# A depthwise convolution with an MLP behind it: how W_in is loaded and cast at the start, and how the taps are spread over the partitions

## The chip, the cores and the metric

One core of one Trainium2 chip. The metric is the device time of one execution in microseconds (us). The engines are named as the profile names them: PE is TensorE (matmuls; PEld its weight loads), DVE is VectorE, ACT is ScalarE, POOL is GpSimd, SP is SyncE, which here only issues DMAs. ACT issues some DMAs too. SPq and ACTq in the trace are those issues.

## The reference

```python
def _attn_ref(x, weight):                 # x [8, 4096, 192], weight [8 heads, 7 taps]
    w = np.exp(weight - max over the taps)
    w = w / (np.sum(w, axis=-1, keepdims=True) + 1e-09)
    x_pad = 6 zero rows ahead of x in each sequence
    out[b, s, h*24 + g] = sum over k of w[h, k] * x_pad[b, s + k, h*24 + g]

def _moe_ref(x, w_in, w_out):             # x [32768, 192], w_in [192, 2048], w_out [2048, 192]
    h = x @ w_in
    g = 0.5 * h * (1.0 + erf(h / sqrt(2)))
    return g @ w_out
```

So each of 8 heads has 7 softmaxed taps, shared by its 24 channels; the causal convolution's result goes through two matrix products with an exact GELU between them.

## The kernel before

The 32768 tokens are cut into two halves of 16384, and the halves run side by side: token half 0 on partitions 0 to 63, half 1 on partitions 64 to 127. The 192 channels lie on those 64 partitions in three groups p = 0, 1, 2 (channel 3i + p on partition i). The tokens of a half are walked in blocks n: six of 256 tokens and then blocks of 512 (`WS`). For a block, 4 DMAs bring x (`load`), DVE transposes it in 32x32 squares (`trans`, L533), the convolution makes `xc` in bf16, PE multiplies by W_in in chunks of 128 columns (`mm1`, L774; in a block of 256, 8 units of two chunks for both halves), ACT takes the GELU of a unit (L694, tile `gT`), and PE multiplies by W_out (`mm2`, L805, and `mm2_t`, L836). PE's order is written out by hand: the `mm2` of block n-1 stand between the `mm1` of block n. `mm1` writes two buffers `hp` by turns, so unit u waits for the GELU of unit u-2.

Blocks 0 and 1 (`PC`) have their convolution on PE: `dg` holds the taps as 7 diagonal 64x64 matrices, and `pconv` (L724) adds up 7 matmuls per group into PSUM; there are four such groups, kinds 0 to 3. ACT and DVE copy the result to `xc` (`conv_out`, L191 and L193). From block 2 on the convolution is on DVE (L559, L566), with `wcol`, the taps as one column of 7 per partition, and from there on DVE works a block ahead of PE.

**W_in.** `win` (bf16) must hold, on each partition half, all 2048 columns. Each half's DMAs bring only 1024 of them, in fp32, into `winf`: half 0 columns 0 to 1023, half 1 columns 1024 to 2047. The 1024 are cut into four quarters s of 256 (`FP`). A DMA `win_in(e, s, hf)` (L234) brings a quarter of one half: 64 partitions with three rows of 256 fp32 each (1 KB), 192 KB. SP issues the four of half 0, ACT the four of half 1; each quarter has a semaphore `S_WIN[s]`, which is at 32 when both halves' DMAs have landed. `own(e, s)` (L222) casts a quarter from `winf` to `win` on all 128 partitions: quarter 0 on DVE (it counts in `S_DUPE`), quarters 1, 2 and 3 on POOL (`S_OWN`). `dup(s, hf)` (L509) on DVE then copies the cast quarter of one half to the other half's partitions, for the columns that it did not load. In block 0 the units 0 to 3 of `mm1` wait for the casts of quarters 0 to 3 and the units 4 to 7 for the doubled ones.

**The order around it.** SP issues the taps' DMA, two loads of block 0's x, four of W_in, the four loads of block 1, four of W_out (`wout_in`), the loads of blocks 2 and 3, and so on. ACT: a dummy Exp (which loads its table), two loads of block 0, the Exp of the taps, a dummy Gelu (L635, which loads that table), four loads of W_in, the casts of block 0 to bf16 (L643), its conv_outs, and then the GELUs. POOL: the identity `idb`, block 0's halo, casts 1 to 3 of W_in, block 1's halo and casts (`cast`, L206), four casts of W_out (`wcast`, L231), and then halos. DVE: the taps, the transposes of block 0, cast 0 of W_in, two conv_outs, the doubling of quarters 0 and 1, the transposes of block 1, the doubling of quarters 2 and 3, block 1's conv_outs, and from there the convolutions.

**The taps.** One DMA (L888) brings `weight` to 64 partitions, each head's 7 taps on 8 of them (a step of 0 in its source). DVE takes the negative maximum (L482), ACT the Exp with its sum (L628), DVE adds 1e-9 (L486), takes the reciprocal (L488) and multiplies (L491, twice, once per half) into `wcol`; L496 makes `dg` from `idb` and `wcol`.

**Block 1's convolution on PE.** `behind` puts 28 of its matmuls behind unit 4 of block 0 and 28 behind unit 5.

Of the kernel before, what the change touches and what calls it, by code (L numbers as in the profile page):

```python
# [11 lines left out]
def bass_lightweight_conv__then__act_gelu_exact_kernel(  # L12
# [84 lines left out]
    def sbt(name, shape, dt):  # L97
        return es.enter_context(nc.sbuf_tensor(name, shape, dt))
# [4 lines left out]
    def sem(name):  # L103
        return es.enter_context(nc.semaphore(name))

    def ap(t, off, pat):
        return bass.AP(t, off, pat)

    with es:
        win = sbt("win", [128, NP * F], BF16)  # L110
        wout = sbt("wout", [128, NF * C], BF16)
        wsb = sbt("wsb", [64, KS], F32)
        wmx = sbt("wmx", [64, 1], F32)
        wsm = sbt("wsm", [64, 1], F32)
        wrc = sbt("wrc", [64, 1], F32)
        wex = sbt("wex", [64, KS], F32)
        wcol = sbt("wcol", [128, KS], F32)
        winf = sbt("winf", [128, NP * F // 2], F32)
        woutf = sbt("woutf", [128, NF * C], F32)
        idb = sbt("idb", [128, 64], BF16)  # L120
# [11 lines left out]
        ob = pst("ob", [128, 2048])  # L132

        S_WSB = sem("S_WSB")
        S_WIN = [sem("S_WIN%d" % i) for i in range(4)]
        S_WOUT = [sem("S_WOUT%d" % i) for i in range(4)]
        S_XIN = [sem("S_XIN%d" % i) for i in range(NX)]
        S_OUT = [sem("S_OUT%d" % i) for i in range(2)]
# [74 lines left out]


        FP = [0, 256, 512, 768, FH]

        WG = [0, 4, 2, 6]

        def own(e, s):

            e.wait_ge(S_WIN[s], 32)
            return e.tensor_copy(  # L222
                ap(win, FP[s], [[NP * F, 128], [F, NP], [1, FP[s + 1] - FP[s]]]),
                ap(winf, FP[s], [[NP * FH, 128], [FH, NP], [1, FP[s + 1] - FP[s]]]),
            )
# [6 lines left out]

        def win_in(e, s, hf):
            e.dma_start(  # L234
                ap(winf, 64 * hf * NP * FH + FP[s], [[NP * FH, 64], [FH, NP], [1, FP[s + 1] - FP[s]]]),
                ap(wint, hf * FH + FP[s], [[NP * F, 64], [F, NP], [1, FP[s + 1] - FP[s]]]),
            ).then_inc(S_WIN[s], 16)

        def wout_in(e, i):
# [166 lines left out]
        @block.gpsimd  # L406
        def _(g):
            g.wait_ge(S_MSET, 1)
            for hf in range(2):
                m = idb[64 * hf : 64 * hf + 64, :]  # L410
                g.affine_select(
                    out=m,
                    in_=m,
                    compare_op=ALU.is_equal,
                    fill=0.0,
                    base=0,
                    pattern=[[-1, 64]],
                    channel_multiplier=1,
                ).then_inc(S_IDN)

            def halo(n):
                if n == 0:

                    t = xTb[0]
                    g.memset(
                        ap(t, 0, [[NP * XB, 128], [XB, NP], [32, HB]]), 0.0
                    ).then_inc(S_HALO)
                    for p in range(NP):
                        g.wait_ge(S_TR, p + 1)
                        g.tensor_copy(  # L430
                            ap(t, p * XB + 1, [[NP * XB, 128], [32, HB], [1, 31]]),
                            ap(
                                xT[0],
                                p * XW + HX + WS[0] - HL,
                                [[NP * XW, 128], [32, HB], [1, 31]],
                            ),
                        ).then_inc(S_HALO)
                    return

                t, tw = (xTb[1], XB) if n in PC else (xT[n % 2], XW)  # L440
                dst = ap(t, HF, [[NP * tw, 128], [tw, NP], [1, HB]])
                if n >= 2:
                    if n - 2 in PC:
                        wait_pc(g, n - 2, NP - 1)
                    else:
                        g.wait_ge(S_CV, cvd(n - 2))
                if OFF[n] % SEQ == 0:
                    g.memset(dst, 0.0).then_inc(S_HALO)
                    return
                g.wait_ge(S_TR, NP * n)  # L450
                if n == 1:
                    src = ap(
                        xT[0],
                        HX + WS[0] - HL + 31,
                        [[NP * XW, 128], [XW, NP], [32, HB]],
                    )
                else:
                    src = ap(
                        xT[(n - 1) % 2],
                        HF + WS[n - 1],  # L460
                        [[NP * XW, 128], [XW, NP], [1, HB]],
                    )
                g.tensor_copy(dst, src).then_inc(S_HALO)  # L463

            g.wait_ge(S_IDN, 2)
            halo(0)
            for s in range(1, 4):
                own(g, s).then_inc(S_OWN)
            halo(1)
            for p in range(NP):  # L470
                cast(g, 1, p)
            for i in range(4):
                wcast(g, i).then_inc(S_WOG)
            for n in range(2, NB):
                halo(n)

        @block.vector
        def _(v):
            v.memset(warm[:, :], 0.0).then_inc(S_WARM)  # L479
            v.memset(idb[:, :], 1.0).then_inc(S_MSET)  # L480
            v.wait_ge(S_WSB, 16)
            v.tensor_reduce(  # L482
                wmx[:, :], wsb[:, :], mybir.AxisListType.X, ALU.max, negate=True
# [3 lines left out]
            v.wait_ge(S_PRO, 2)  # L487
            v.reciprocal(wrc[:, :], wsm[:, :]).then_inc(S_PRO)  # L488
            v.wait_ge(S_PRO, 3)
            for hf in range(2):  # L490
                v.tensor_scalar(  # L491
                    wcol[64 * hf : 64 * hf + 64, :], wex[:, :], wrc[:, 0:1], None, ALU.mult
                ).then_inc(S_PRO)
            v.wait_ge(S_PRO, 5)
            v.wait_ge(S_IDN, 2)
            v.tensor_tensor(  # L496
                ap(dg, 0, [[KS * 64, 128], [64, KS], [1, 64]]),
                ap(idb, 0, [[64, 128], [0, KS], [1, 64]]),
                ap(wcol, 0, [[KS, 128], [1, KS], [0, 64]]),
                ALU.mult,  # L500
            ).then_inc(S_DG)

            def dup(s, hf):

                if s == 0:
                    v.wait_ge(S_DUPE, 1)
                else:
                    v.wait_ge(S_OWN, s)
                v.tensor_copy(  # L509
                    ap(  # L510
                        win,
                        64 * (1 - hf) * NP * F + FH + FP[s],
                        [[NP * F, 64], [F, NP], [1, FP[s + 1] - FP[s]]],
                    ),
                    ap(
                        win,
                        64 * hf * NP * F + FP[s],
                        [[NP * F, 64], [F, NP], [1, FP[s + 1] - FP[s]]],
                    ),
                ).then_inc(S_DUPE)  # L520
# [65 lines left out]

            for p in range(NP):
                trans(0, p)
            own(v, 0).then_inc(S_DUPE)
            conv_out(v, 0, 1)  # L590
            conv_out(v, 0, 4)
            for s in range(2):
                for hf in range(2):
                    dup(s, hf)
            for p in range(NP):
                trans(1, p)
            for s in range(2, 4):
                for hf in range(2):
                    dup(s, hf)
            for j in range(len(PIECES)):  # L600
                conv_out(v, 1, j)

# [18 lines left out]
        def _(a):  # L621
# [10 lines left out]
                bias=wmx[:, 0:1],  # L632
                accum_out=wsm[:, 0:1],
            ).then_inc(S_ACTP)
            a.activation(  # L635
                out=hot[:, 1:2], in_=nc.const_aps.tensor(0.0, (1, 1), F32), func=AF.Gelu
            ).then_inc(S_HOT)
            for s in range(4):
                win_in(a, s, 1)
            a.wait_ge(S_PRO, 5)  # L640
            for p in range(NP):
                a.wait_ge(S_TR, p + 1)
                a.activation(  # L643
# [61 lines left out]
        def _(t):  # L705
# [33 lines left out]
            for kd in order:  # L739
                pconv(*seq[kd].pop(0))  # L740

            behind = {
                (0, 4): [(1, kd, k) for k in taps for kd in (0, 1)],
                (0, 5): [(1, kd, k) for k in taps for kd in (2, 3)],
            }

            def mm1(n, i):
# [7 lines left out]
                    else:  # L755
                        t.wait_ge(S_CV, cvd(n))
                if n == 0:
                    if 1 <= i < 4:
                        t.wait_ge(S_OWN, i)
                    else:  # L760
                        t.wait_ge(S_DUPE, 1 if i == 0 else 2 * (i - 4) + 3)
                for cc in range(c):
                    for p in range(NP):
                        if n in PC and i == 0 and cc == 0 and p == NP - 1:
# [119 lines left out]

        @block.sync
        def _(sp):

            sp.dma_start(  # L888
                wsb[:, :], ap(wt, 0, [[KS, H], [0, 64 // H], [1, KS]])
            ).then_inc(S_WSB, 16)  # L890
            load(sp, 0, (0, 1))
            for s in range(4):
                win_in(sp, s, 0)
            load(sp, 1)
            for i in range(4):
                wout_in(sp, i)
            load(sp, 2)
            load(sp, 3)
            for n in range(1, NB):
                if n + 3 < NB:  # L900
                    load(sp, n + 3)
                store(sp, n - 1)
            for g in range(NG[NB - 1]):
                store_half(sp, g, 0)
            for s in range(2):
                sp.wait_ge(S_OUT[s], OUTS[NB - 1 if (NB - 1) % 2 == s else NB - 2])
# [28 lines left out]
```

## Time and profile before

| | |
|---|---|
| median of 6 runs | 686.67 us (686.03 to 688.16) |
| the profiled execution | 686.24 us, its span 684.5 us |
| mean granted PE clock in the span | 0.997 |
| PE busy | 676.8 us |
| L774 (mm1), busy | 420.9 us |
| L836 (mm2_t), busy | 366.3 us |
| L694 (GELU on ACT), busy | 523.3 us |
| L222 on POOL, L222 on DVE: one cast of a quarter | 0.83 us, 0.69 us |
| W_in, issue to landing, median: on SP, on ACT | 4.8 us, 6.5 us |

The groups of L774 and L836 overlap in PE's pipeline, so that their sum is more than PE's busy time. The page gives totals over the whole span; what happens in the first 30 us, which is where everything that the change touches lies, is read from the timeline and from the chain of waits. In a timeline line stand the start, the length, the engine, the line of the program, the operation, what it writes and reads, how many instructions the line stands for, and in brackets how long the engine had been idle before it and what ended that.

### The profile page before, as it was taken

What the parts mean: (1) busy time and instruction counts of PE and PEld (TensorE: products, weight loads), DVE (VectorE), ACT (ScalarE), POOL (GpSimd) and SP (SyncE); (2) the same over time, 40 slices, a digit from 0 to 9 for tenths busy, and PEclk for the clock granted to TensorE, in tenths of its full rate; (3) what the DMA queues carried; (4) which work ended last, traced back from release to release, by engine and by line L of the source; (5) the groups of instructions that cost most, each with busy time, mean ns of one, the idle gap of its engine ahead of it and who ended that gap; (6) DMA issues with size and microseconds to landing.
All of it is one profiled execution on the core that took longest, in us unless ns stands there. A gap on an engine that the chain in (4) does not pass through costs nothing.

```text
span 684.5 us, 27321 instructions
## 1 busy us (share of the span) xinstructions
PE 676.8 (99%) x12576; PEld 411.4 (60%) x12576; DVE 560.3 (82%) x902; ACT 537.2 (78%) x550; POOL 37.4 (5%) x54
## 2 busy tenths in 40 slices
PE   7999999999999999999999999999999999999998
PEld 4899755555555555555555555555555555555556
DVE  4899979888898888898888898888898888988611
ACT  5799987877777877788777877777878777778772
POOL 3224200000000000000000000000000000000000
PEclk9999999999999999999999999999999999999999
DMA  8445421244422344422344422444322444321223
GB/s 213 105 115 112 101 60 36 61 94 95 95 60 57 73 94 95 94 59 52 82 94 95 90 50 56 91 94 95 82 48 62 95 94 95 70 47 29 48 49 94
DMA packets 134363, 55.23 MB, mean 81 GB/s; under 512 B 127593, under 2 KB 134249, under 8 KB 134249
## 3 DMA queue, kind: packets, MB, share of 16 engines
q1 hardware_dynamic: 132296, 52.12, 34.7%
q8 instruction: 98, 1.61, 0.9%
q10 hardware_dynamic: 1952, 1.38, 0.8%
q14 instruction: 17, 0.13, 0.1%
HBM read 28.31 MB, written 25.17 MB: 78 GB/s over the span
## 4 chain that ended last, share of the span: by engine, by line
PE 95%; ACT 2%; DMA 1%; DVE 1%; issue 0%; POOL 0%; ACTq 0%
PE hp L774 47%; PE ob L836 42%; PE ob L805 5%; ACT gT L694 1%; DMA winf<-in_moe_w_in_dram 1%; DMA wsb<-in_weight_dram 0%; DVE xc L193 0%; PE ob L724 0%; ACT L635 0%; ACT osb L297 0%; DVE osb L339 0%; POOL win L222 0%; DVE osb L308 0%; ACT wex L628 0%; DVE wmx L482 0%
## 5 line engine op out<-in xcount | busy, mean ns | idle before, releaser
L694 ACT ACTIVATE gT<-hp 128x1024 bf16<-128x1024 f32 x512 | 523.3, 1024 | 131.5 <-PE hp L774 128.3
L774 PE MATMUL hp<-xc,win 64*64 64x512 bf16 (+2 forms) x6048 | 420.9, 366 | 2.8 <-POOL win L222 1.3
L836 PE MATMUL ob<-gT,wout 64*64 64x512 bf16 x5376 | 366.3, 376 | 0.0
L566 DVE SCALAR_TENSOR_TENSOR acc<-xT,wcol,acc 128x512 f32<-128x512 f32 (+1 forms) x495 | 314.7, 704 | 0.0
L774 PEld LDWEIGHTS hp<-xc,win 64*64 64x64 bf16 (+1 forms) x6048 | 191.0, 106 | 136.6 <-issue 1.7
L836 PEld LDWEIGHTS ob<-gT,wout 64*64 64x64 bf16 x5376 | 172.2, 118 | 122.7
L339 DVE STREAM_TRANSPOSE osb<-ob 128x512 f32<-128x512 f32 x84 | 74.0, 884 | 101.8 <-PE ob L836 101.8
L533 DVE STREAM_TRANSPOSE xT<-xin 128x512 f32<-128x512 f32 (+1 forms) x105 | 78.2, 796 | 4.0 <-DMA xin<-in_x_dram 4.0
L566 DVE SCALAR_TENSOR_TENSOR xc<-xT,wcol,acc 128x512 bf16<-128x512 f32 (+1 forms) x99 | 65.3, 717 | 0.0
L463 POOL COPY xT<-xT 128x18 f32<-128x18 f32 x30 | 27.9, 928 | 505.1 <-DVE xT L533 482.8
L805 PE MATMUL ob<-wout,gT 64*128 64x192 bf16 x1024 | 52.9, 243 | 0.3
L805 PEld LDWEIGHTS ob<-wout,gT 64*128 64x128 bf16 x1024 | 44.9, 94 | 5.2 <-PE ob L805 0.6
L559 DVE TENSOR_SCALAR acc<-xT,wcol 128x512 f32<-128x512 f32 (+1 forms) x90 | 37.6, 473 | 1.1
L310 ACT ACTIVATE osb<-ob 128x192 f32<-128x192 f32 x4 | 1.3, 332 | 9.5 <-PE ob L805 9.5
L308 DVE COPY osb<-ob 128x192 f32<-128x192 f32 x4 | 1.4, 358 | 8.4 <-PE ob L805 8.4
L708 PE MATMUL hp<-warm 128*128 128x512 bf16 x16 | 5.4, 510 | 1.3 <-DVE warm L479 1.3
L297 ACT ACTIVATE osb<-ob 128x384 f32<-128x384 f32 x12 | 5.8, 486 | 0.0
L667 ACT ACTIVATE acc<-xT,wcol 128x256 f32<-128x256 f32 (+1 forms) x9 | 5.2, 574 | 0.0
L509 DVE COPY win<-win 64x768 bf16<-64x768 bf16 x8 | 4.1, 515 | 0.9 <-POOL win L222 0.7
L708 PEld LDWEIGHTS hp<-warm 128*128 128x128 bf16 x16 | 1.9, 126 | 4.2 <-issue 2.4
L724 PE MATMUL ob<-xTb,dg 64*64 64x256 bf16 (+1 forms) x112 | 3.2, 245 | 0.5 <-ACT xTb L643 0.5
L231 POOL CAST wout<-woutf 128x768 bf16<-128x768 f32 x4 | 3.4, 870 | 1.9 <-DMA woutf<-in_moe_w_out_dram 1.9
(29 smaller groups left out, 20.2 us busy)
## 6 DMA issues: line engine op xcount, KB each, us to landing
out_dram<-osb SPq DMA_DIRECT2D x122, 192.0 KB, 3.6
xin<-in_x_dram SPq DMA_DIRECT2D x116, 192.0 KB, 4.1
xin<-in_x_dram SPq DMA_DIRECT2D x22, 96.0 KB, 5.6
woutf<-in_moe_w_out_dram SPq DMA_DIRECT2D x4, 384.0 KB, 9.0
winf<-in_moe_w_in_dram SPq DMA_DIRECT2D x4, 192.0 KB, 4.8
winf<-in_moe_w_in_dram ACTq DMA_DIRECT2D x4, 192.0 KB, 6.5
out_dram<-osb SPq DMA_DIRECT2D x8, 48.0 KB, 1.9
out_dram<-osb ACTq DMA_DIRECT2D x4, 96.0 KB, 2.0
```

The source lines that it names most:

```text
L297: e.activation(out=dst, in_=src, func=AF.Copy).then_inc(S_EVA)
L339: v.transpose(ap(osb[m % 2], j, [[8 * C, 128], [C // 2, TB // 32], [NP, 32]]), bank(ring(m, j)),).then_inc(S_EV)
L463: g.tensor_copy(dst, src).then_inc(S_HALO)
L533: v.transpose(ap(xT[n % 2], p * XW + HX, [[NP * XW, 128], [1, w]]), ap(xin[n % NX], p, [[TB // 32 * DQ, 128], [DQ, w // 32], [NP, 32]],),) ...
L559: ins = v.tensor_scalar(a, src, wk, None, ALU.mult)
L566: ins = v.scalar_tensor_tensor(dst, src, wk, a, op0=ALU.mult, op1=ALU.add)
L667: a.activation(out=acc[n % 2][:, p * TB : p * TB + w], in_=ap(xT[n % 2], p * XW + HX, [[NP * XW, 128], [1, w]]), func=AF.Copy, scale=wcol[ ...
L694: a.activation(out=ap(gT[n % 2], i * c * 2 * w, dst), in_=ap(hp[u % 2], 0, src), func=AF.Gelu,).then_inc(S_GELU)
L708: t.matmul(hp[1][:, 0:512], warm[:, 0:128], warm[:, :])
L774: ins = t.matmul(hp[u % 2][fo : fo + fw, o : o + w], ap(win, f1, [[NP * F, 64], [2, fw]]), xc[n % 2][r, p * TB : p * TB + w], start=(p == ...
L805: ins = t.matmul(bank(bb[sub], w=C), gT[m % 2][r, c0 : c0 + 128], wout[r, CH[sub][i] * C : (CH[sub][i] + 1) * C], start=(ph == 0 and i == ...
L836: ins = t.matmul(bank(ring(m, j), slice(64 * h, 64 * h + 64), w), ap(wout, 64 * hf * NF * C + CH[h][i] * C + j, [[NF * C, 64], [NP, 64]],) ...
```

## The change

- W_in comes in two parts s per half instead of four quarters: `FW` is 512 columns, so a DMA has rows of 2 KB and 384 KB in all. SP and ACT issue two each. There are two semaphores `S_WIN`; quarters 0 and 1 wait for the first, 2 and 3 for the second. On ACT the two stand ahead of the dummy Gelu instead of behind it.
- The four casts are still quarters. POOL has 0, 2 and 3 (in this order, `S_OWN`), DVE has quarter 1 (`S_DUPE`), after its two conv_outs of block 0 instead of ahead of them. The waits of `mm1` and `dup` follow.
- DVE doubles quarters 0, 1 and 2 ahead of block 1's transposes and quarter 3 behind them.
- The taps' DMA brings 8 partitions, one per head. Their softmax runs on 8 partitions, into the corner of a zeroed 32x32 tile `wnm`; a transpose makes `wnt` (taps on partitions, heads in columns), and four transposes, whose source takes each of four head columns eight times over, write `wcol` on 32 partitions each. `wcol` gets 32 columns, of which 7 are used.
- Block 1's convolution on PE stands behind units 5 and 6 instead of 4 and 5.

The core of the diff:

```diff
-        S_WIN = [sem("S_WIN%d" % i) for i in range(4)]
+        S_WIN = [sem("S_WIN%d" % i) for i in range(2)]
...
+        FW = FH // 2
...
         def own(e, s):
-            e.wait_ge(S_WIN[s], 32)
+            e.wait_ge(S_WIN[s // 2], 32)
...
         def win_in(e, s, hf):
             e.dma_start(
-                ap(winf, 64 * hf * NP * FH + FP[s], [[NP * FH, 64], [FH, NP], [1, FP[s + 1] - FP[s]]]),
-                ap(wint, hf * FH + FP[s], [[NP * F, 64], [F, NP], [1, FP[s + 1] - FP[s]]]),
+                ap(winf, 64 * hf * NP * FH + FW * s, [[NP * FH, 64], [FH, NP], [1, FW]]),
+                ap(wint, hf * FH + FW * s, [[NP * F, 64], [F, NP], [1, FW]]),
             ).then_inc(S_WIN[s], 16)
...
             halo(0)
-            for s in range(1, 4):
+            for s in (0, 2, 3):
                 own(g, s).then_inc(S_OWN)
...
+            v.memset(wnm[:, :], 0.0).then_inc(S_MSET)
...
-            for hf in range(2):
-                v.tensor_scalar(
-                    wcol[64 * hf : 64 * hf + 64, :], wex[:, :], wrc[:, 0:1], None, ALU.mult
+            v.wait_ge(S_MSET, 2)
+            v.tensor_scalar(
+                wnm[0:H, 0:KS], wex[:, :], wrc[:, 0:1], None, ALU.mult
+            ).then_inc(S_PRO)
+            v.wait_ge(S_PRO, 4)
+            v.transpose(wnt[:, :], wnm[:, :]).then_inc(S_PRO)
+            v.wait_ge(S_PRO, 5)
+            for q in range(4):
+                v.transpose(
+                    wcol[32 * q : 32 * q + 32, :],
+                    ap(wnt, 4 * (q % 2), [[32, 32], [1, 4], [0, 8]]),
                 ).then_inc(S_PRO)
-            v.wait_ge(S_PRO, 5)
+            v.wait_ge(S_PRO, 9)
...
             for p in range(NP):
                 trans(0, p)
-            own(v, 0).then_inc(S_DUPE)
             conv_out(v, 0, 1)
             conv_out(v, 0, 4)
-            for s in range(2):
+            own(v, 1).then_inc(S_DUPE)
+            for s in range(3):
                 for hf in range(2):
                     dup(s, hf)
             for p in range(NP):
                 trans(1, p)
-            for s in range(2, 4):
-                for hf in range(2):
-                    dup(s, hf)
+            for hf in range(2):
+                dup(3, hf)
...
+            for s in range(2):
+                win_in(a, s, 1)
             a.activation(
                 out=hot[:, 1:2], in_=nc.const_aps.tensor(0.0, (1, 1), F32), func=AF.Gelu
             ).then_inc(S_HOT)
-            for s in range(4):
-                win_in(a, s, 1)
-            a.wait_ge(S_PRO, 5)
+            a.wait_ge(S_PRO, 9)
...
             behind = {
-                (0, 4): [(1, kd, k) for k in taps for kd in (0, 1)],
-                (0, 5): [(1, kd, k) for k in taps for kd in (2, 3)],
+                (0, 5): [(1, kd, k) for k in taps for kd in (0, 1)],
+                (0, 6): [(1, kd, k) for k in taps for kd in (2, 3)],
             }
...
-            sp.dma_start(
-                wsb[:, :], ap(wt, 0, [[KS, H], [0, 64 // H], [1, KS]])
-            ).then_inc(S_WSB, 16)
+            sp.dma_start(wsb[:, :], ap(wt, 0, [[KS, H], [1, KS]])).then_inc(S_WSB, 16)
             load(sp, 0, (0, 1))
-            for s in range(4):
+            for s in range(2):
                 win_in(sp, s, 0)
```

More of the change, by code (lines that the diff above doesn't have):

```diff
@@ L111, in bass_lightweight_conv__then__act_gelu_exact_kernel @@
         wout = sbt("wout", [128, NF * C], BF16)
[L112 to L117, printed above, removed]
+        wsb = sbt("wsb", [H, KS], F32)
+        wmx = sbt("wmx", [H, 1], F32)
+        wsm = sbt("wsm", [H, 1], F32)
+        wrc = sbt("wrc", [H, 1], F32)
+        wex = sbt("wex", [H, KS], F32)
+        wnm = sbt("wnm", [32, 32], F32)
+        wnt = sbt("wnt", [32, 32], F32)
+        wcol = sbt("wcol", [128, 32], F32)
         winf = sbt("winf", [128, NP * F // 2], F32)
@@ L498, in _ @@
                 ap(idb, 0, [[64, 128], [0, KS], [1, 64]]),
-                ap(wcol, 0, [[KS, 128], [1, KS], [0, 64]]),
+                ap(wcol, 0, [[32, 128], [1, KS], [0, 64]]),
                 ALU.mult,
@@ L503, in dup @@
             def dup(s, hf):
-                if s == 0:
+                if s == 1:
                     v.wait_ge(S_DUPE, 1)
                 else:
-                    v.wait_ge(S_OWN, s)
+                    v.wait_ge(S_OWN, max(1, s))
                 v.tensor_copy(
@@ L757, in mm1 @@
                 if n == 0:
-                    if 1 <= i < 4:
-                        t.wait_ge(S_OWN, i)
+                    if i < 4 and i != 1:
+                        t.wait_ge(S_OWN, max(1, i))
                     else:
-                        t.wait_ge(S_DUPE, 1 if i == 0 else 2 * (i - 4) + 3)
+                        t.wait_ge(S_DUPE, 1 if i == 1 else 2 * (i - 4) + 3)
                 for cc in range(c):
```

## The prediction

> **What bounds the kernel now.** I read the page's totals first, then the chain of waits over the first 90 us, then the timeline of the first 33 us engine by engine, then a table by stage.
>
> ```profile
> span 684.5 us, 27321 instructions
> PE 676.8 (99%) x12576; PEld 411.4 (60%) x12576; DVE 560.3 (82%) x902; ACT 537.2 (78%) x550; POOL 37.4 (5%) x54
> ```
>
> TensorE (PE) works for 676.8 of 684.5 us, so 7.7 us is all that its idle time can give. The chain of waits says where it lies; columns are start, length, what:
>
> ```profile
> 0.81 2.53 DMA wsb<-in_weight_dram
> ...
> 4.03 1.17 ACT L635
> 5.20 0.03 issue
> 5.23 6.85 DMA winf<-in_moe_w_in_dram
> 12.08 0.05 issue
> 12.13 0.84 POOL win L222
> 12.97 0.14 issue
> 13.11 1.48 PE hp L774 x12
> ```
>
> Up to 13.1 us the end is set by the transfer of W_in and one cast of it on GpSimd (POOL); from 21.04 us on the chain is PE matmuls one after another. The timeline gives the PE gaps up to there in brackets: 0.48, 0.91, 0.88, 0.43, 0.17 and 0.22 us, 3.09 together. Of the rows around them:
>
> ```profile
> 8.41 0.69 DVE L222 CAST win<-winf 128x768 bf16<-128x768 f32 x1 [1.61 <-DMA winf<-in_moe_w_in_dram]
> ...
> 10.52 0.83 POOL L222 CAST win<-winf 128x768 bf16<-128x768 f32 x1 [3.32 <-DMA winf<-in_moe_w_in_dram]
> ...
> 12.13 0.83 POOL L222 CAST win<-winf 128x768 bf16<-128x768 f32 x1 [0.78 <-DMA winf<-in_moe_w_in_dram]
> ...
> 13.31 0.83 POOL L222 CAST win<-winf 128x768 bf16<-128x768 f32 x1 [0.35 <-DMA winf<-in_moe_w_in_dram]
> ```
>
> Each of the four casts starts when its quarter of W_in lands: 8.4, 10.5, 12.1, 13.3 us, so 1.63 us a quarter (393 KB), 241 GB/s. What comes behind is late for the same reason:
>
> ```profile
> 22.50 1.34 DVE L533 STREAM_TRANSPOSE xT<-xin 128x256 f32<-128x256 f32 x3 [1.52 <-DMA xin<-in_x_dram]
> ...
> 30.62 1.26 DVE L566 SCALAR_TENSOR_TENSOR xc<-xT,wcol,acc 128x256 bf16<-128x256 f32 x3
> ...
> 32.03 0.83 PE L774 MATMUL hp<-xc,win 64*128 64x256 bf16 x12
> ```
>
> Block 2's input lands at 22.50; VectorE (DVE) then works without a pause to 31.88, and PE starts that block at 32.03. The slack is 0.15 us: PE can't gain more than the landing of block 2's x gains, plus 0.15. In block 3 the slack is also small (xc done at 42.41, matmuls from 42.56). The stage table shows what the DMA engines could do (after the stretch and its length: busy PE, PEld, DVE, ACT, POOL; granted clock; DMA share; GB/s):
>
> ```profile
> 7.50:10.50 3.00, 2.09 (x66) 1.59 (x60) 2.00 (x5) 1.47 (x5) 0.00 (x0) 1.00 1.00 233
> 10.50:13.30 2.80, 1.49 (x17) 0.83 (x17) 1.01 (x3) 1.60 (x2) 1.66 (x2) 0.70 1.23 231
> 15.00:17.50 2.50, 2.33 (x53) 1.59 (x50) 2.41 (x6) 2.50 (x3) 2.15 (x5) 0.99 1.09 377
> ```
>
> W_in with its 1 KB rows moves at about 232 GB/s, W_out with 1.5 KB rows (15 to 17.5 us) at 377, both with the DMA engines full (share 1.0 and more).
>
> **The change, part by part.**
>
> *W_in in two parts of 2 KB rows.* Four issues fewer (two on SP, two on ACT, about 0.6 us each); the bytes are the same. Call T the time of one quarter's bytes, and let the first land at 8.4 minus (1.63 - T). Part A is complete one T after it, part B three T. With T 1.63 (the rate of before) A lands at 10.0 (the trace has 10.5 for its second quarter) and B at 13.3. With W_out's rate T is 393/377 = 1.04: first quarter 7.8, A 8.8, B 10.9, so 2.4 us saved at the end. A 2 KB row is longer than both, but its pitch in memory is W_in's and not the contiguous one of W_out, so I stand between: T = 1.3, A 9.4, B 12.0, 1.3 saved; the bounds are 0 and 2.4. The taps' transfer has 8 rows in place of 64. Its issue took 0.79 us and the small stores of L377 (64 rows) took 0.32 at the least; everything behind it on SP moves up by 0 to 0.47, I take 0.2. So A 9.2, B 11.8, and all that stands behind W_in on SP (x of block 1, W_out, x of block 2) lands 1.5 earlier (bounds 0 to 2.9): x of block 2 at 21.0.
>
> [...]
>
> *The taps.* Two multiplications L491 go (0.48). One multiplication on 8 rows comes (0.24) and five 32x32 transposes. The trace has no transpose of 32 columns: below it stands the smallest DVE row, 0.15, above it the 128x256 one of L533, 1.32/3 = 0.44. It is nearer to the small one: 0.18. Net 0.24 + 0.90 - 0.48 = +0.66 (0.51 to 1.96). The new memset (0.11, by L480) lies in DVE's 2.09 us wait for the taps. The taps land earlier, 0 to 0.79, I take 0.3. So dg ends at 5.9 instead of 5.56, the first transposes of x end at 7.2 instead of 6.79. On ACT the first cast waited until 6.63 though its input was there at 5.9: the four W_in issues held its sequencer until 6.53. Now two issues (to about 4.6) stand ahead of the table load (1.28 + 0.20, to 6.1), so casts start at 6.4 and the last follows the last transpose, at 7.6 (7.66 before). The convolution of block 0 ends near 8.7 as before: zero, covered by A, which lands later than that. Without cover, at 1.96, xc of block 0 would be ready at about 10.9, 0.8 on PE's path.
>
> *Casts moved.* GpSimd takes quarter 0, then 2 and 3; DVE quarter 1. On DVE the two copies to xc (9.13, 0.64) no longer stand behind a cast (0.69), so they end at 9.4. GpSimd: cast 0 from 9.2 to 10.05; 2 and 3 wait for the whole of B, 11.8 to 12.65 to 13.5. Behind these on GpSimd stand block 1's halo and casts and the W_out casts; behind cast 1 on DVE (9.4 to 10.1) the doubling copies (0.43 each) and block 1's transposes. PE then: chunk 0 at 10.1 (9.66 before), 1 at 10.8 (11.41), 2 at 12.7 (13.11), 3 at 13.6 (14.6). From here the GELU sets the pace, 1.02 each with two buffers: chunk 4 at 14.5, 5 at 15.6.
>
> *Block 1's convolution one chunk later on PE.* PE: first half 16.2 to 17.1 (0.89), chunk 6, second half to 18.3 (0.53), chunk 7 to 18.95; DVE's six copies (2.30) start at 17.1 and end at 19.3; block 1's first chunk ends at 19.65 against 21.65. PE gains 2.0. The clock: before, 12 to 15 us ran at a granted 0.50 after the gaps. If a gap at 8.7 to 10.1 does that again, chunks 2 and 3 take 1.3 instead of 0.66, some 0.6 later: gain 1.4.
>
> [...]
>
> *The sum.* PE reaches block 2 by 1.4 to 2.0 us earlier, DVE's xc by 1.5 (21.0 + 9.38 = 30.4) with 0.15 slack. W_out's last cast ends at 20.4 (21.94 - 1.5), needed at 20.6. So 1.6 us less: 686.24 (the profiled execution: span 684.5 and 1.7 around it) becomes 684.6. The median of the runs stands 0.43 above that execution, so 685.1.
>
> **The rivals.**
> 1. The saving is hidden: T stays 1.63, A 10.5, B 13.3, x of block 2 at 22.3. GpSimd's casts 2 and 3 then end at 14.1 and 15.0 (12.97 and 14.14 before), chunk 2 is a microsecond later, and the later place of block 1's convolution makes up for it: 21.5 against 21.65. 0 to 0.35 less: 686.5. For it: the DMA share is already 1.0. Against: 377 GB/s at the same share.
> 2. More: W_out's rate, T 1.04, 2.6 to 2.9 less, near the 3.09 of gaps: 683.9. Against: PE then needs W_out's last cast and DVE just as early.
> 3. Slower: the coarse wait. Casts 2 and 3 can't begin before all of B is there, and they run one after the other (0.83 each) with eight GELUs behind. By the steps above, a landing at 13.9 gives the old time and every microsecond past it costs one; from 15.3 on it is slower by more than a measurement can tell. For it: SP's x loads of block 1 are issued 1.2 us earlier and share the engines with ACT's half of B (231 GB/s with a share of 1.23 at 10.5 to 13.3). Against: the three quarters after the first would have to move at 170 GB/s (1.18 MB from 8.4 to 15.3). With B at 15.5: 688.2.
>
> **How the numbers follow.** Forecast 0.45 (its own range 684.3 to 685.8, T from 1.1 to 1.5), rival 1 0.29, rival 2 0.15, rival 3 0.11. 0.2%, about what a measurement of this kernel can tell, is 1.37 us: faster is below 685.3. That takes rival 2 and 0.37 of the forecast, 0.52; slower is rival 3 and 0.01, 0.12; the rest 0.36. The range reaches from 683.4 (all gaps gone) to 686.9 (rival 1 with a little loss).
>
> **What would show it.** Right: quarters' casts on GpSimd at about 9.2, 11.8 and 12.65; W_in above 290 GB/s; block 2's transposes at 21.0; block 1's first chunk near 19.7; PE still back to back from there. The taps' part: dg ending at 5.7 to 6.1. Wrong: x of block 2 still at 22.5 (rival 1, with a new PE gap ahead of block 2), B past 13.9 (rival 3), or transposes of 0.4 us, which would push the first convolution past A.

## The result and the profile after

| | before | after |
|---|---|---|
| median of all runs, us | 686.88 (37 runs, 685.94 to 689.27) | 688.67 (16 runs, 687.10 to 689.99) |
| the profiled execution, its span, us | 686.24, 684.5 | 687.67, 685.9 |
| PE busy / idle in the span, us | 676.8 / 7.7 | 677.1 / 8.8 |
| mean granted PE clock | 0.997 | 0.995 |

The ratio of after to before is 1.0023 with an interval of 1.0014 to 1.0031: the change costs about 1.8 us. The profiled execution of after is one of its shorter ones, 1.4 us above that of before.

The totals on the page of after:

```profile
span 685.9 us, 27323 instructions
PE 677.1 (99%) x12576; PEld 410.2 (60%) x12576; DVE 561.2 (82%) x907; ACT 537.4 (78%) x550; POOL 37.5 (5%) x54
```

PE does the same 12576 matmuls. Its idle time is 1.1 us more and its busy time 0.3 us, which is the span's 1.4. The chain of waits of after (start, length, what) says where:

```profile
3.31 10.42 DMA winf<-in_moe_w_in_dram
13.73 0.05 issue
13.79 0.84 POOL win L225
14.63 0.14 issue
14.76 4.69 PE hp L787 x48
19.45 0.95 PE ob L737 x28
```

The transfer of W_in still sets the end, and it ends at 13.73 us; before, the third quarter (the last that the chain needed) was there at 12.08. The chain's next link, one cast on GpSimd, is the same 0.84. The timeline of after, in which PE's four chunks 2 to 5 are the 4.69 us line, shows what hangs on it:

```profile
10.15 0.69 DVE L225 CAST win<-winf 128x768 bf16<-128x768 f32 x1 [1.80 <-DMA winf<-in_moe_w_in_dram]
10.18 1.08 POOL L225 CAST win<-winf 128x768 bf16<-128x768 f32 x1 [3.23 <-DMA winf<-in_moe_w_in_dram]
...
11.41 2.60 PE L787 MATMUL hp<-xc,win 64*128 64x256 bf16 x24 [3.44 <-POOL win L225]
...
13.79 1.60 POOL L225 CAST win<-winf 128x768 bf16<-128x768 f32 x2 [2.52 <-DMA winf<-in_moe_w_in_dram]
...
14.76 4.69 PE L787 MATMUL hp<-xc,win 64*128 64x256 bf16 x48 [0.75 <-POOL win L225]
...
23.23 1.34 DVE L547 STREAM_TRANSPOSE xT<-xin 128x256 f32<-128x256 f32 x3 [0.56 <-DMA xin<-in_x_dram]
...
31.34 1.27 DVE L580 SCALAR_TENSOR_TENSOR xc<-xT,wcol,acc 128x256 bf16<-128x256 f32 x3
...
33.53 0.82 PE L787 MATMUL hp<-xc,win 64*128 64x256 bf16 x12
```

Part A starts the casts at 10.15 (the prediction has 9.2), part B at 13.79 (11.8). PE's gaps are 3.44 and 0.75, 4.19 together against 3.09 before. Block 2's `xc` is done at 32.61, 0.7 us later than before, but PE takes that block up only at 33.53, 1.5 us later than the 32.03 of before: PE itself is late now, and its 1.5 is the span's 1.4. In the stage table of after (stretch and length; busy PE, PEld, DVE, ACT, POOL with their instructions; granted clock; DMA share; GB/s) stands the reason:

```profile
7.00:10.00 3.00, 0.98 (x50) 0.81 (x40) 0.63 (x2) 1.31 (x5) 0.00 (x0) 1.00 0.98 225
10.50:13.30 2.80, 1.89 (x20) 1.74 (x22) 2.03 (x5) 0.53 (x1) 0.77 (x1) 0.70 1.20 191
15.00:17.50 2.50, 2.50 (x26) 1.76 (x24) 2.43 (x5) 1.10 (x2) 1.36 (x4) 0.50 1.06 359
```

W_in with its 2 KB rows moves at 225 GB/s, no faster than with 1 KB rows (215 in the same stretch before, 233 in 7.5 to 10.5), while W_out still moves at 359. The 191 of the second row isn't the rate of W_in: in 10.5 to 13.3 us the DMA view of after has 895 packets with 0.53 MB, and 765 of them are under 512 B, rows of block 1's x of 384 B each, which is more than half of the bytes. The same holds for the 231 that the prediction has from this stretch before (1010 of 1285 packets). The clock is at 0.50 in 15 to 17.5; before, it had returned to 0.99 there. The other half of the change, the taps, in the timeline of after:

```profile
2.17 0.15 DVE L486 TENSOR_REDUCE wmx<-wsb 8x1 f32<-8x7 f32 x1 [0.87 <-DMA wsb<-in_weight_dram]
...
3.46 0.20 DVE L501 STREAM_TRANSPOSE wnt<-wnm 32x32 f32<-32x32 f32 x1
3.70 0.90 DVE L504 STREAM_TRANSPOSE wcol<-wnt 32x32 f32<-32x32 f32 x4
4.63 0.63 DVE L510 TENSOR_TENSOR dg<-idb,wcol 128x448 bf16<-128x448 bf16 x1
...
6.54 1.44 PE L737 MATMUL ob<-xTb,dg 64*64 64x256 bf16 x56
```

The taps land at 2.17 instead of 3.37, `dg` is done at 5.26 instead of 5.56, and block 0's convolution ends at 7.98 instead of 8.75. None of it counts here, because PE then waits 3.44 us for W_in.

### The profile page after: what moved, and what is told of

It reads as the page before. It is cut to its first block, busy times and chain, and to the rows that moved or that the text cites. A ratio compares the mean times of both kernels' runs of the same rounds, so it can differ in the third digit from the quotient of the medians.

```text
span 685.9 us, 27323 instructions
## 1 busy us (share of the span) xinstructions
PE 677.1 (99%) x12576; PEld 410.2 (60%) x12576; DVE 561.2 (82%) x907; ACT 537.4 (78%) x550; POOL 37.5 (5%) x54
## 3 DMA queue, kind: packets, MB, share of 16 engines
q10 hardware_dynamic: 1536, 1.38, 0.9%
## 4 chain that ended last, share of the span: by engine, by line
PE 95%; DMA 2%; ACT 1%; DVE 0%; issue 0%; SPq 0%; POOL 0%; DVEq 0%
PE hp L787 47%; PE ob L849 42%; PE ob L818 5%; DMA winf<-in_moe_w_in_dram 2%; ACT gT L707 1%; DVE xc L195 0%; SPq L358 0%; ACT osb L300 0%; PE ob L737 0%; DVE osb L342 0%; POOL win L225 0%; SPq L237 0%; SPq L900 0%; DVE osb L311 0%; DVEq L202 0%
## 5 line engine op out<-in xcount | busy, mean ns | idle before, releaser
L195 DVE CAST xc<-ob 64x256 bf16<-64x256 f32 (+3 forms) x8 | 2.8, 356 | 3.3 <-PE ob L737 3.1
```

## The experiments

Each kernel ran beside the kernel before on the same chip, and the ratios are to that; before_taps, before_win2, after_fill and before_fill shared one chip, after_q4, after_fill2 and the two contig kernels a second, after_q4pair, after_again and the two 128 kernels a third, and the other four a fourth. A column "A, B" gives the starts of the first and of the third cast of W_in in the profiled execution. In the two 128 kernels the third cast stood directly behind another on GpSimd, so that B says less of the landing there.

| run | median, before beside it | ratio (95%) | A, B | span |
|---|---|---|---|---|
| before_taps | 686.46, 687.33 | 0.9989 (0.9979 to 0.9998) | 7.5, 10.1 | 683.5 |
| taps_again | 685.97, 686.65 | 0.9980 (0.9968 to 0.9991) | 7.8, 11.1 | 684.7 |
| before_win2 | 688.46, 687.33 | 1.0019 (1.0011 to 1.0028) | 11.9, 14.0 | 686.0 |
| after_q4 | 685.92, 686.64 | 0.9995 (0.9983 to 1.0008) | 7.7, 10.9 | 684.1 |
| after_q4pair | 686.90, 687.21 | 0.9993 (0.9981 to 1.0004) | 10.2, 13.6 | 685.5 |
| after_fill | 687.96, 687.33 | 1.0011 (1.0002 to 1.0020) | 11.6, 14.4 | 686.8 |
| before_fill | 686.80, 687.33 | 0.9997 (0.9988 to 1.0006) | 9.8, 12.4 | 684.9 |
| after_fill2 | 687.86, 686.64 | 1.0013 (1.0004 to 1.0021) | 11.3, 14.3 | 686.5 |
| after_fill2b | 688.32, 686.65 | 1.0020 (1.0006 to 1.0034) | 10.9, 14.3 | 687.7 |
| after_again | 688.94, 687.21 | 1.0024 (1.0013 to 1.0035) | 11.7, 15.4 | 688.5 |
| after_third | 688.47, 686.65 | 1.0024 (1.0013 to 1.0035) | 10.6, 14.0 | 686.9 |
| after_contig | 687.3, one run | | 9.5, 12.9 | 685.6 |
| before_contig | 685.9, one run | | 9.1, 11.8 | 684.1 |
| after_128 | 686.35, 687.21 | 0.9987 (0.9975 to 1.0000) | 10.3, 11.3 | 684.7 |
| before_128 | 686.16, 687.21 | 0.9982 (0.9968 to 0.9996) | 7.2, 11.3 | 684.5 |
| after_rows1k | 687.58, 686.65 | 1.0011 (1.0002 to 1.0020) | 9.7, 13.4 | 685.9 |

### Each half of the change alone

before_taps is the kernel before with only the taps of the change:

```diff
-    wcol[64 * hf : 64 * hf + 64, :], wex[:, :], wrc[:, 0:1], None, ALU.mult   (two halves)
+    wnm[0:H, 0:KS], wex[:, :], wrc[:, 0:1], None, ALU.mult
+    v.transpose(wnt[:, :], wnm[:, :])
+    for q in range(4): v.transpose(wcol[32 * q : 32 * q + 32, :], ...)
-    wsb[:, :], ap(wt, 0, [[KS, H], [0, 64 // H], [1, KS]])
+    wsb[:, :], ap(wt, 0, [[KS, H], [1, KS]])
```

> The kernel before with the taps' part of the change alone (8 partitions, five transposes). Clock theory (the change is slower because PE stands idle for 3.4 us while part A of W_in is in flight, and then runs at half clock to 18.4 us): the taps are innocent, dg ends 0.3 us earlier and W_in's DMAs start 0.4 us earlier, so 686.3 to 686.9. Transfer theory (the loss is only that the 2 KB parts land late): the same. Rival, the taps are at fault: 688 or more.

before_win2 is the kernel before with only the loads of the change; the casts, their engines and block 1's convolution stay as before:

```diff
-    for s in range(4): win_in(a, s, 1)     # SP the same
+    for s in range(2): win_in(a, s, 1)     # rows of 2 KB
-    e.wait_ge(S_WIN[s], 32)
+    e.wait_ge(S_WIN[s // 2], 32)
```

> The kernel before with the two-part loads of W_in alone, casts and their engines as before. Both the clock and the transfer theory: slower, 688 to 689, first cast at 10 to 10.5 us instead of 8.4, part B at 13.3 to 14; the clock theory adds half clock past 15 us. Rival, the moved casts, the taps or the later place of block 1's convolution are at fault: 686.9, as before.

The taps alone are faster (0.9989), the loads alone slower (1.0019): the loss is in the loads. The casts in the timeline of before_taps:

```profile
7.49 0.67 DVE L224 CAST win<-winf 128x768 bf16<-128x768 f32 x1
...
8.83 0.83 POOL L224 CAST win<-winf 128x768 bf16<-128x768 f32 x1 [0.74 <-DMA winf<-in_moe_w_in_dram]
...
10.14 0.83 POOL L224 CAST win<-winf 128x768 bf16<-128x768 f32 x1 [0.48 <-DMA winf<-in_moe_w_in_dram]
...
11.68 0.83 POOL L224 CAST win<-winf 128x768 bf16<-128x768 f32 x1 [0.71 <-DMA winf<-in_moe_w_in_dram]
```

and in that of before_win2:

```profile
11.89 0.69 DVE L223 CAST win<-winf 128x768 bf16<-128x768 f32 x1 [4.41 <-DMA winf<-in_moe_w_in_dram]
11.92 1.08 POOL L223 CAST win<-winf 128x768 bf16<-128x768 f32 x1 [4.04 <-DMA winf<-in_moe_w_in_dram]
...
13.96 1.65 POOL L223 CAST win<-winf 128x768 bf16<-128x768 f32 x2 [0.96 <-DMA winf<-in_moe_w_in_dram]
```

With the old loads the quarters come 1.3 to 1.5 us apart. With the new ones nothing is there until 11.9. The taps were run again to see whether their gain holds:

> The kernel before with the taps' part alone, once more: 0.3 to 1.2 us under the kernel before, 2 us or more under the changed kernel.

Its sign holds (0.9980), though each of the two gains, 0.11 and 0.20%, is no more than the 0.2% that I count as telling.

### Is it the clock?

The half clock of after (granted 0.50) lasts from 11.6 to 18.4 us, that of before from 11.6 to 15.05. The theory was that the 3.44 us gap brings it on and that chunks 2 to 5 (1.17 us each, against the GELU's 1.02) pay for it. Matmuls on a zero tile fill the gap:

```diff
+            for _ in range(14):                    # ahead of chunk 0
+                t.matmul(hp[1][:, 0:512], warm[:, 0:128], warm[:, :])
...
+                    for _ in range({2: 8}.get(i, 0)):   # ahead of chunk 2
+                        t.matmul(bank(3), warm[:, 0:128], warm[:, :])
```

> The changed kernel with 14 matmuls on zeros ahead of block 0's first chunk and 8 ahead of its third, in time in which PE waits. Clock theory: the granted clock stays at 1.0, chunks 2 to 5 take 0.66 us instead of 1.2, and the time falls by 1 to 2 us to 686.7 to 687.7. Transfer theory: part B (13.7 us) and block 2's x (23.2 us) still set the end, 688.3 to 689.

before_fill does the same to the kernel before, with 4, 4, 4 and 2 of them ahead of chunks 0 to 3:

> The kernel before with 4, 4, 4 and 2 matmuls on zeros in PE's gaps ahead of chunks 0 to 3 of block 0. Clock theory: no half clock at 11.6 to 15, at most 0.15 us gained unless block 2's x comes earlier, since PE reached block 2 only 0.15 us after its xc: 686.6 to 686.9. Transfer theory: the same. Rival (the fillers cost PE time of their own): 687.5.

before_fill is as the kernel before (0.9997). In after_fill the clock was 1.0 throughout, yet only 0.12 points of the loss went. My 8 fillers were badly placed: they stood behind the wait for the GELU and held chunk 2 up to 16.61 us. after_fill2 has 14 and, ahead of that wait, 4:

> The changed kernel with 14 matmuls on zeros ahead of block 0's first chunk and 4 behind its second chunk, the latter ahead of the wait for the GELU, so that they don't stand between a landed part B and the third chunk. Clock theory: granted clock 1.0 and 0.7 to 1.5 us under the changed kernel, 687.0 to 687.8. Transfer theory: no less than 688.3.

> The changed kernel with the fillers of after_fill2. If half clock is a part of the loss: 0.6 to 1.2 us under the changed kernel of this call, and still 0.5 us or more above the kernel before, because the late landings stay. If it is none: within 0.4 us of the changed kernel.

1.0013 and 1.0020 on two chips: 687.86 lies between what the two theories had (at most 687.8, at least 688.3), and 688.32 gives the clock next to nothing. To judge that, the changed kernel itself was run again on two chips, after_third beside after_fill2b:

> The changed kernel once more, beside the next on one chip: 1.5 to 2 us above the kernel before; part A's landing between 10 and 12 us.

> The changed kernel beside the next three on one chip: 1.5 to 2 us above the kernel before.

Both gave 1.0024, and the profiled execution of after_third had no half clock at all: in 15 to 18.5 us the window table of after has

```profile
15.00:18.50 3.50, 3.50 (x36) 2.37 (x32) 3.27 (x7) 2.06 (x3) 2.35 (x6) 0.51 1.06 360
```

and that of after_third

```profile
15.00:18.50 3.50, 3.06 (x48) 2.15 (x48) 3.38 (x7) 2.61 (x3) 2.35 (x6) 1.00 1.06 351
```

At full clock PE did 48 matmuls there instead of 36, and still this execution was one of 688.62 us. The theory falls as the whole cause: the filled kernels, at full clock, stay 0.63, 1.22 and 1.67 us above the kernel before on their chips (the changed kernel 1.73 to 1.82), so the ratio is lower by 0.04 (on the same chip) to 0.13 points, within the intervals. As a part of it the clock isn't ruled out. Of the 40 executions of the changed kernel (16, and 12 each in after_again and after_third), the nine with a clock of 0.999 or more are on average 1.0 us above the median of the kernel before beside them, and the other 31 are 2.0 us above it. As a late W_in both lengthens the gap and delays PE, this doesn't tell the cost of the clock from that of the landing. In after_third, what the full clock gained is lost again a little later, as its timeline shows:

```profile
20.81 0.50 PE L787 MATMUL hp<-xc,win 64*128 64x256 bf16 x5
...
22.75 1.25 PE L787 MATMUL hp<-xc,win 64*128 64x256 bf16 x19 [1.44 <-issue]
```

PE stood idle for 1.44 us in the midst of a chunk, with nothing to wait for in the profile. It does so in other executions, some at full clock throughout (1.95 us in after_fill2b, 1.03 in after_q4) and some with a half clock earlier on (1.01 in taps_again, 0.98 in before_128), and the timeline of after_fill2b has it 17 matmuls earlier in the program:

```profile
20.59 0.42 PE L737 MATMUL ob<-xTb,dg 64*64 64x128 bf16 x16
...
22.96 0.36 PE L737 MATMUL ob<-xTb,dg 64*64 64x128 bf16 x12 [1.95 <-issue]
```

That kernel has 18 matmuls more ahead of this place, so the gap stands at nearly the same place in PE's stream of instructions. In after_third a transfer of 16 KB on the instruction queue ran from 20.03 to 21.37, and PE, which stopped at 21.31, went on 1.38 us after its end. The other traces bear this out: in all seven that have the gap (0.36 to 1.95 us), PE goes on 1.25 to 1.51 us after the end of such a transfer, and in the eleven that don't, PE comes to this place 1.39 us or more after it. So in every trace PE passes this place no sooner than 1.25 us after that transfer's end. That the transfer causes the gap is my reading and not shown, as no run moved the transfer by itself.

### Is it the coarse wait, or the moved casts?

after_q4 takes the changed kernel back to quarters of 1 KB rows with a semaphore each; casts, taps and convolution stay as changed:

```diff
-        FW = FH // 2
+        FW = FH // 4
-            e.wait_ge(S_WIN[s // 2], 32)
+            e.wait_ge(S_WIN[s], 32)
-            for s in range(2): win_in(a, s, 1)     # SP the same
+            for s in range(4): win_in(a, s, 1)
```

> The changed kernel with W_in again in four quarters of 1 KB rows with four semaphores; taps, casts, their engines, ACT's order and block 1's convolution stay as changed. Theory (the 2 KB parts are the whole loss): about as the taps alone, 0.0 to 1.0 us under the kernel before, first cast near 7.5 us, no half clock or one window of it. Rival, the moved casts or the later convolution cost something of their own: 0.5 us or more above the kernel before.

after_q4pair has the same quarters, but two of them on one semaphore, so that casts 2 and 3 wait for all of the second half as in the change:

```diff
-            e.wait_ge(S_WIN[s // 2], 32)
+            e.wait_ge(S_WIN[s // 2], 64)           # quarters of 1 KB rows
...
-            ).then_inc(S_WIN[s], 16)
+            ).then_inc(S_WIN[s // 2], 16)
```

> The changed kernel with 1 KB rows in eight DMAs again, but with its two semaphores: casts 0 and 1 wait for quarters 0 and 1 together, casts 2 and 3 for 2 and 3. If the coarse wait is the loss: near the changed kernel, 1.2 us or more above the kernel before. If the slower move of the 2 KB rows (packets of 160 ns, both halves at once) is the loss: A at 9.0 to 9.5, B at 12.3 to 12.8, and at most 0.5 us above the kernel before. Partly both: in between.

0.9995 and 0.9993: the loss is gone with the quarters, and the coarse wait brings nothing of it back (686.90 against the 688.94 of after_again on the same chip). So rival 3's mechanism isn't the cause. But the landings that I expected for after_q4pair (9.0 to 9.5 and 12.3 to 12.8) were missed; its timeline has

```profile
10.25 1.08 POOL L225 CAST win<-winf 128x768 bf16<-128x768 f32 x1 [3.28 <-DMA winf<-in_moe_w_in_dram]
...
13.63 1.60 POOL L225 CAST win<-winf 128x768 bf16<-128x768 f32 x2 [2.29 <-DMA winf<-in_moe_w_in_dram]
```

which is where the profiled execution of after has them (10.18 and 13.79), and that execution is one of the shorter ones of after. So the medians show that the quarters take the loss away, and these two profiles don't show how. What does differ in them is the clock in 15 to 17.5 us (1.00 here, 0.50 in after). The moved casts and the later place of block 1's convolution cost nothing that shows either: after_q4 (0.9995) has them and before_taps and taps_again (0.9989, 0.9980) don't, with overlapping intervals.

### Is it the pitch in memory?

after_contig and before_contig let every W_in DMA read one contiguous piece, with everything else as it was:

```diff
-   ap(wint, hf * FH + FW * s, [[NP * F, 64], [F, NP], [1, FW]]),
+   ap(wint, (2 * s + hf) * 64 * NP * FW, [[NP * FW, 64], [FW, NP], [1, FW]]),
```

> The changed kernel, but each W_in DMA reads 393 KB that lie together in memory (64 x 3 rows of 2 KB one behind the other) instead of rows 8 KB apart; W_in's values are then in the wrong places, so the product is another matrix's. If the 8 KB pitch in memory sets the rate: W_in moves at 330 GB/s or more, A lands by 8.5 and B by 10.5. If the side of the 64 partitions sets it: A at 10 to 12 and B at 13 to 14.5, as in the changed kernel.

> The same for the kernel before: each quarter's DMA reads 197 KB that lie together (rows of 1 KB); the product is another matrix's. Pitch: the four casts start by about 7.5, 8.5, 9.5 and 10.5. Partition side: 8.4, 10.5, 12.1, 13.3 as before.

A at 9.5 and B at 12.9 (10.2 to 11.7 and 13.8 to 15.4 in the executions of the changed kernel), and 9.1 and 11.8 for before (8.4 and 12.1): a little earlier at most, and far from what 377 GB/s would bring (8.8 and 10.9 by the prediction's steps). With one run each, a small part of the pitch in the landing can't be told from the spread between executions, but the pitch isn't what keeps W_in from the rate of W_out.

### Is it the 64 partitions?

W_out's DMAs write 128 partitions, W_in's 64. after_128 loads each part with one DMA over all 128 (rows of 2 KB), before_128 each quarter (1 KB):

```diff
-   ap(winf, 64 * hf * NP * FH + FW * s, [[NP * FH, 64], [FH, NP], [1, FW]]),
-   ap(wint, hf * FH + FW * s, [[NP * F, 64], [F, NP], [1, FW]]),
+   ap(winf, 512 * s, [[NP * FH, 128], [FH, NP], [1, 512]]),
+   ap(wint, 128 * NP * 512 * s, [[NP * 512, 128], [512, NP], [1, 512]]),
...      (SP brings part A, ACT part B; each cast waits for one DMA, 16, instead of two)
```

> The changed kernel with one DMA of 786 KB per part that writes all 128 partitions with 2 KB rows (from memory that lies together, W_in's values in the wrong places, so the product is another matrix's); SP brings part A, ACT part B. If the half of the partitions sets the rate: 330 GB/s or more as with W_out, A by 7.5, B by 9.5, packets under 100 ns, and 2 us or more under the changed kernel. If long rows as such are slow: A after 9, B after 12.

> The same in quarters of 1 KB rows on 128 partitions, SP quarters 0 and 2, ACT 1 and 3, the rest as in the kernel before (another matrix's product): partition theory, casts at 6.5 to 9.5 instead of 8.4 to 13.3 and 1.5 us or more under the kernel before, if block 2's x comes earlier too. Otherwise as before.

The DMA view of after in 7 to 10 us (packets, bytes and rate; then for each queue packets, MB and the share of 16 engines' time that they took; q10 is ACT's, q1 SP's):

```profile
DMA packets 355, 0.67 MB, mean 225 GB/s; under 512 B 26, under 2 KB 26, under 8 KB 355
...
q10 hardware_dynamic: 174, 0.34, 51.1%
q1 hardware_dynamic: 181, 0.34, 47.1%
```

and of after_128 in 5.5 to 8.5 us:

```profile
DMA packets 582, 1.16 MB, mean 386 GB/s; under 512 B 16, under 2 KB 16, under 8 KB 582
...
q1 hardware_dynamic: 304, 0.62, 54.4%
q10 hardware_dynamic: 278, 0.54, 48.6%
```

The engines are equally full. The time of a 2 KB packet is its queue's share times 16 engines times 3 us over its packets: on q10 0.511 x 48 / 174 = 141 ns with 64 partitions, 0.486 x 48 / 278 = 84 ns with 128 (on q1 125 and 86). So the same number of bytes in rows of the same length moves 1.7 times as fast (386 against 225 GB/s) when one DMA spans all partitions; before_128 has 343 GB/s with 1 KB rows in 5.5 to 8 us. This is the difference that I had read off W_in and W_out and put down to the rows. The landings that I expected were missed even so: in after_128 part B was there 6.1 us after its issue at 2.46, before part A, which shared the engines with it and landed 7.6 us after 2.67, at 10.3 instead of 7.5. All of W_in is there by then, 3.4 us earlier than in after. In before_128 the last cast starts at 12.64 instead of 9.5, and the time is 1.05 us under before, not 1.5. Both kernels have a ratio below 1 (0.9987, with an interval up to 1.0000, and 0.9982), though they read W_in from places that give another product. No kernel here loads W_in itself in this way: its halves need source addresses that don't go on evenly from partition 63 to 64.

In 7 to 10 us of after the two queues fill opposite halves of the partitions at the same time (51.1% and 47.1%), and together they have 225 GB/s, against the 386 of two DMAs that each span all 128. So here a second DMA at work on the other half didn't make up for the 64 partitions of the first. The rate is shown and its reason isn't.

### Row length, or the size of a DMA?

after_rows1k keeps the four DMAs of 384 KB and the two semaphores, and cuts only the rows to 1 KB (six per partition):

```diff
-   ap(winf, 64 * hf * NP * FH + FW * s, [[NP * FH, 64], [FH, NP], [1, FW]]),
-   ap(wint, hf * FH + FW * s, [[NP * F, 64], [F, NP], [1, FW]]),
+   ap(winf, 64 * hf * NP * FH + 256 * s, [[NP * FH, 64], [512, 6], [1, 256]]),
+   ap(wint, hf * 512 + 256 * s, [[NP * F, 64], [FH, 6], [1, 256]]),
...      (the casts take the quarters in the order 0, 2, 1, 3, in which these rows fill them)
```

> The changed kernel, its four W_in DMAs of 384 KB and its two semaphores, but each DMA moves 6 rows of 1 KB per partition instead of 3 of 2 KB (the rows go to other places of the tile, so the product is another matrix's). If it is the length of the rows: packets of 70 to 80 ns, as after_q4pair, at most 0.4 us above the kernel before. If it is the size or the small number of the DMAs: A and B as late as in the changed kernel and 1.2 us or more above the kernel before.

1.0011 against 1.0024 of after_third on the same chip: by the medians about half of the loss goes with the rows, and the other half stays with the few large DMAs. The intervals overlap, and 0.93 us above before lies between the two outcomes that I had set (0.4 and 1.2), so how it splits stays open. The DMA view of after_rows1k in 7 to 10 us:

```profile
DMA packets 646, 0.64 MB, mean 213 GB/s; under 512 B 22, under 2 KB 646, under 8 KB 646
...
q10 hardware_dynamic: 372, 0.37, 67.4%
```

0.674 x 48 / 372 = 87 ns for a 1 KB packet: a kilobyte takes 87 ns in short rows and 141 / 2 = 71 in long ones, and yet the mean rate is no higher with the long ones (225 against 213 in these stretches). Here, on 64 partitions, the length of the rows doesn't set the rate. What goes with it in the traces is the size of the DMAs: in 7 to 10 us the four kernels with the changed taps and quarters of 192 KB (before_taps, taps_again, after_q4, after_q4pair) moved 244 to 296 GB/s, and the changed kernel's three executions, with DMAs of 384 KB, 225 to 230.

One more rival: with two loads fewer ahead of it, SP issues the loads of block 1's x from 4.06 us on instead of 5.62, and they share the engines with the end of W_in. But in 10.5 to 13.3 us after moved 765 of their short packets, and after_q4pair, which has no loss, 993. Nothing points to it, though no run held these loads back.

## Why the prediction was wrong

It had 685.1 us and gave "slower" 0.12; the runs have 688.67.

- **The step that failed** is "T = 1.3, A 9.4, B 12.0, 1.3 saved", and in it the reading of W_out's 377 GB/s as what longer rows can reach. The rate of W_out goes with its 128 partitions (W_in's bytes on 128: 386 in after_128 with 2 KB rows, 343 in before_128 with 1 KB), and W_in on 64 had no such reserve (225). The prediction named length and pitch as what may set the two apart and left the partitions out. A landed for the casts at 10.2 to 11.7 and B at 13.8 to 15.4 in three executions of the changed kernel.
- **The lower bound of that step** was wrong too. I took "0 saved" as the worst, with T as before and B at 13.3. Two large DMAs of 2 KB rows landed later than that, and nothing in my bounds let the transfer itself get slower. Longer rows gained nothing: W_in had 225 GB/s with 2 KB rows, and 215 to 233 with 1 KB rows before.
- **Rival 3** has the outcome: B at 13.8 in one profiled execution and past its 13.9 in the two others. Its price, one microsecond for each past that point, has the right direction and the wrong level: B at 13.8, 14.0 and 15.4 goes with spans of 685.9, 686.9 and 688.5, while by the price they would be 684.4, 684.6 and 686.0. Its mechanism, the coarse wait, is refuted by after_q4pair (0.9993); the transfer came later of itself, once past the 15.3 that I had held to be too late. That the outcome had a place among the rivals is luck: it came by another way.
- **The clock.** The price of 0.6 us for a half clock was meant for chunks 2 and 3. In after it lasted until chunk 5, and chunks 2 to 5 took 4.69 us from 14.76 on; at full clock they took 3.69 in after_third (15.01 to 18.70). So of the 1.5 us by which the span of after lies above rival 3's price, 1.0 is the clock's. In after_third another gap of 1.44 us took its place. How much of the median's loss is the clock's stays open.
- **The slack at block 2** stopped being the limit. I had PE and DVE bound together there; with W_in later, PE came 0.9 us behind DVE (33.53 against 32.61).
- **The taps** were right in kind and too small in size: transposes 0.20 and 0.225 (I took 0.18), but the landing came 1.2 us earlier where I took 0.3, so `dg` ended at 5.26 instead of 5.9. "Zero, covered by A" held in the changed kernel. In before_taps and taps_again A starts at 7.5 and 7.8, and there the same taps gain 0.11 and 0.20%: they are what the change has of use.
- **"Casts moved"** and **"block 1's convolution one chunk later"** were right as far as that they do no harm that shows. The 2.0 us that I expected of the latter never came to be seen, because chunk 2 was 2 us later than assumed (14.76 against 12.7).

The fastest versions here that compute the reference are the taps alone, 0.9989 and 0.9980 of before, ahead of both kernels.

Two things stay open: how the loss divides between row length, DMA size and the half clock (0.50 in 15 to 17.5 us of after, none in after_third), and why the landing of the same kernel moves by 1.5 us from one execution to the next (A 10.2 to 11.7, B 13.8 to 15.4), which is as much as the loss itself. A single profile for each kernel therefore places the loss; its size rests on the medians.

## What to carry to other kernels

Before a faster transfer is priced from the rate of another one, compare everything in which the two differ: here row length, pitch and the number of partitions all differed, and only the last one made the difference of 225 to 386 GB/s. With the DMA engines full (share 0.98 in 7 to 10 us of after), a bound of "nothing gained" wasn't the lower one: it had part B at 13.3 us, and with four DMAs of 384 KB in place of eight of 192 KB part B landed at 13.8 to 15.4. And a change of two parts should be priced, and run, as two.

## What the runs showed of the hardware that was not expected

- 2 KB packets took 141 ns in DMAs over 64 partitions and 84 ns over 128, at equal share of the engines (225 against 386 GB/s), though two queues filled opposite halves at once.
- A cast of a quarter on GpSimd took 1.08 us where a cast on VectorE (0.69) ran beside it, in after, after_again and before_win2, and 0.83 alone; VectorE's was not slowed.
- PE stood idle for 0.36 to 1.95 us with nothing to wait for in the profile, at nearly the same place in its instruction stream, in seven of 18 traces, and went on 1.25 to 1.51 us after a 16 KB transfer on the instruction queue had ended.
- A 3.44 us gap at the start was followed by a half clock (0.50 from 11.6 to 18.4 us) in one execution of after, a 2.77 us gap (after_third) by none (1.00 from 11 to 21.3 us), and a 2.52 us gap (after_rows1k) by a half clock again (0.50 in 15 to 17.5). The length of the gap alone doesn't decide it.
